# Filler products of the first batch, placed anew

## The chip, the cores and the metric

The kernel runs on one core of a Trainium2 chip. A core has five engines with an instruction queue each: TensorE (matrix products; PE in the profile, PEld its weight loads), VectorE (DVE), ScalarE (ACT), GpSimd (POOL) and SyncE (SP, which here only issues transfers). The metric is the time of one execution on the device in microseconds (us), lower is better; the time of a kernel is the median of several executions.

## The reference

It is a retention layer followed by a Fourier mixing block, for batch 4, 8 heads, 768 positions and head size 64:

```python
# attention: a decaying state for each head, y = scale * q . state
gamma = 1.0 - 2.0 ** (-5.0 - np.arange(H))
for t in range(S):
    state = gamma[None, :, None, None] * state + einsum('bhd,bhe->bhde', k[:, :, t], v[:, :, t])
    y[:, :, t] = scale * einsum('bhd,bhde->bhe', q[:, :, t], state)
x = y.transpose(0, 2, 1, 3).reshape(B, S, H * D)      # 4 x 768 x 512
# mixing and a two-layer network
u = x + real(fft(fft(x, axis=1), axis=2))
un = (u - mean(u)) / sqrt(var(u) + 1e-6)
out = u + maximum(un @ w_ch1, 0) @ w_ch2              # 512 -> 2048 -> 512
```

## The kernel before

The four batches go through the same stages one after the other. In the attention of a batch the eight heads are four pairs, numbered 0 to 3, and the 768 positions are six chunks of 128. The Fourier transforms are products with cosine and sine tables (`csp`, `ssp`, `cd16`, `sd16`), which the kernel computes itself at the start. Then comes the network, in halves of 384 rows.

While a later batch's attention runs, TensorE has the network of the batch before as dense work. The first batch has nothing of that kind beside it: its attention runs while the inputs arrive and while the tables are made. Its work is therefore written out by hand as one long list, `first_units()` (L1216): each entry is a small unit that issues some instructions on one engine, and `pin()` (L108) makes every engine keep exactly the order of the list. So a unit on an engine waits for all units of that engine that stand ahead of it, and beyond that only for its inputs and for free buffers.

The units that matter here, in the order in which a pair passes through them:

- `q0_unit`, `k0_unit`, `v0_unit` (L436 to L472) convert a pair's loaded q, k and v to 16 bits; the last letter names the engine (P for GpSimd, V for VectorE, A for ScalarE). The twelve loads themselves (L189) stand in SyncE's queue from the start.
- `t0_unit(i, part)` (L483): six TensorE transposes of q (part 0) or k (part 1); `te_unit` (L492, L495) copies the result, qTz or kT, out of PSUM on ScalarE or VectorE.
- `am_unit(i, half)` (L509): six products kT with qT into two wkA tiles; `ae_unit` (L516, VectorE) scales and masks them into atm.
- `kv0_unit` (L531): ten products of k and v into wkK; `sc_unit` (L540, VectorE) scans them into the running state s.
- `yi_unit` (L559) and `yx_unit` (L571): the products with atm and with the state that make y (wkY); `x0_unit` (L337, L339) writes y, scaled, to x.
- `trig` and `t_act` (L301 to L330) build the tables between these units, on ScalarE, VectorE and GpSimd; `mir_s`, `mir_d`, `turn_d` mirror them.
- `fold_s`, `fold_d`, `s1a_pre`, `s1b_pre`, `s1_mm`, `s1a_fin`, `s1b_fin` (L724, L738, L791, L839): the folds of x and the first Fourier products, after which TensorE's dense work begins (`px_unit`, `s2e_unit`, `h0_unit`, `ch_unit`).
- `w1_unit` and `w2_unit` (L1167, L1174) issue the eight transfers of the network's weights from GpSimd's queue. The loads of batch 1 (`load_unit`, L169) stand in SyncE's queue behind the seventh of them and behind a product of the first batch's network.

A filler is a product that nobody reads: `filler(n)` (L152) multiplies a tile of zeros, 128 x 128 by 128 x 512, n times into a PSUM tile of its own, `wps`. It waits for nothing but the zeros, written once at the start, and nothing waits for it, except the TensorE instructions that stand behind it in the queue. Six fillers are issued ahead of the list (L215), and six single ones stand in the list.

Of the kernel before, what the change touches and what calls it, by code (L numbers as in the profile page):

```python
# [18 lines left out]
P = 128  # L19
# [26 lines left out]
def kernel(  # L46
# [105 lines left out]
    def filler(n):  # L152
        def run():
            for _ in range(n):
                nc.tensor.matmul(wps, wz[:, 0:P], wz, start=True, stop=True)
        return run
# [138 lines left out]
    def trig(idx, part, eng):  # L295
        n, w, c = (S, SW, idx) if idx < 3 else (DM, DW, idx)
        r, ra = rs[2 * idx][:, 0:w], rs[2 * idx + 1][:, 0:w]

        def run():
            if part == 0 and eng == "A":  # L300
                nc.scalar.activation(ra, kf[:, 0:w], AF.Copy, bias=MAGIC, scale=icoln[:, c:c + 1])  # L301
            elif part == 0:
                eng_of(eng).tensor_scalar(out=ra, in0=kf[:, 0:w], scalar1=icoln[:, c:c + 1],
                                          scalar2=MAGIC, op0=ALU.mult, op1=ALU.add)
            elif part == 1:
                eng_of(eng).tensor_scalar(out=ra, in0=ra, scalar1=-MAGIC, scalar2=float(n),
                                          op0=ALU.add, op1=ALU.mult)
            else:
                eng_of(eng).scalar_tensor_tensor(out=r, in0=kf[:, 0:w], scalar=icol[:, c:c + 1],
                                                 in1=ra, op0=ALU.mult, op1=ALU.subtract)  # L310
        return run
# [124 lines left out]
    def q0_unit(i):  # L436
        def run():
            q16 = q16_of[0, i] = qzs[i % 2].rearrange("p h c d -> p (h c d)")[
                :, 0:NCH * P].rearrange("p (c h d) -> p c h d", c=NCH, h=2)
            nc.gpsimd.tensor_scalar(out=q16, in0=in_of.pop(("q", 0, i)).rearrange(  # L440
                "p h c d -> p c h d"), scalar1=1.0, scalar2=1.0, op0=ALU.mult, op1=ALU.mult)
        return run

    def k0_unit(i, h2, eng="P"):
        def run():
            h = 2 * PAIR_ORDER[i] + h2
            if h2 == 0:
                kd_of[0, i] = kp.tile([P, NCH, 2, D], f16, tag="kd16", name="kd16")
            k32, kd = in_of["k", 0, i][:, h2], kd_of[0, i][:, :, h2, :]
            if eng == "A":  # L450
                nc.scalar.activation(kd, k32, AF.Copy, bias=0.0, scale=gkd[:, h:h + 1])
            else:
                (nc.vector if eng == "V" else nc.gpsimd).tensor_scalar(
                    out=kd, in0=k32, scalar1=gkd[:, h:h + 1], scalar2=1.0, op0=ALU.mult,
                    op1=ALU.mult)
        return run
# [17 lines left out]
    def t0_unit(i, part):  # L474
        def run():
            if part == 0:
                at[0, i] = dict(kT=tp.tile([P, NCH, P], f16, tag="kT", name="kT"),
                                qT=qts[i % 2][:, 0])
            src = (q16_of, kd_of)[part][0, i]
            tq = at[0, i]["tq", part] = ps_g.tile([P, NCH, P], f16, tag="g", name="tq",  # L480
                                                  padded_shape=[P, 8, P])
            for c in range(NCH):
                nc.tensor.transpose(tq[:, c, :], src[:, c].rearrange("p a b -> p (a b)"), ident16)  # L483
        return run
# [730 lines left out]

    def first_units():  # L1216
        return [
            filler(1), trig(0, 0, "V"), trig(2, 0, "A"), k0_unit(0, 0, "V"), trig(1, 0, "V"),
            k0_unit(0, 1, "A"), q0_unit(0), t0_unit(0, 0), t0_unit(0, 1), te_unit(0, 0, "A"),
            filler(1), icoln_unit, te_unit(0, 1, "V"), am_unit(0, 0), trig(3, 0, "A"),  # L1220
            trig(4, 0, "A"), trig(4, 1, "P"), trig(2, 1, "P"), q0_unit(1), t0_unit(1, 0),
            trig(0, 1, "V"), k0_unit(1, 0, "P"), gk_unit(0), trig(0, 2, "V"), trig(2, 2, "V"),
            t_act(2, 0), k0_unit(1, 1, "A"), trig(1, 1, "P"), ae_unit(0, 0, 1), am_unit(0, 1),
            trig(4, 2, "V"), t_act(4, 2), v0_unit(0, 0, 6, "P"), parity_a, t_act(2, 2),
            filler(1), t0_unit(1, 1), trig(1, 2, "V"), kv0_unit(0), v0_unit(1, 0, 6, "P"),
            ae_unit(0, 1, 1), yi_unit(0, 1), t_act(0, 0), t_act(2, 1), sc_unit(0),
            te_unit(1, 1, "A"), te_unit(1, 0, "A"), am_unit(1, 0), am_unit(1, 1), t_act(0, 1),
            trig(3, 1, "V"), q0_unit(2), ae_unit(0, 1, 0), gk_unit(1), filler(1), kv0_unit(1),
            ae_unit(1, 0, 1), trig(3, 2, "V"), x_edges(1), t_act(4, 0), ae_unit(0, 0, 0),
            ae_unit(1, 1, 0), sc_unit(1), t_act(3, 2), yi_unit(0, 0), k0_unit(2, 0, "A"),  # L1230
            yx_unit(0), x0_unit(0, 0, "A"), t0_unit(2, 0), x0_unit(0, 1, "A"),
            k0_unit(2, 1, "P"), t0_unit(2, 1), te_unit(2, 1, "A"), ae_unit(1, 1, 1), yx_unit(1),
            te_unit(2, 0, "V"), t_act(1, 0), q0_unit(3), mir_d(1, "P"), t_act(1, 1),
            ae_unit(1, 0, 0), yi_unit(1, 0), x0_unit(1, 0, "V"), am_unit(2, 0), ae_unit(2, 0, 1),
            yi_unit(1, 1), x0_unit(1, 1, "A"), am_unit(2, 1), t0_unit(3, 0), ae_unit(2, 1, 0),
            mir_s(0, "P"), ae_unit(2, 1, 1), filler(1), te_unit(3, 0, "V"),
            fold_s(0, 0, 258, 0, 1, (1,), "V"), k0_unit(3, 0, "A"), k0_unit(3, 1, "P"),
            t0_unit(3, 1), te_unit(3, 1, "A"), am_unit(3, 0), w1_unit(0), v0_unit(2, 0, 3, "P"),
            fold_s(0, 0, 258, 0, 1, (0,), "V"), ae_unit(2, 0, 0), filler(1),
            v0_unit(2, 3, 6, "A"), minus_unit("A"), kv0_unit(2), t_act(3, 0), yi_unit(2, 0),  # L1240
            am_unit(3, 1), ae_unit(3, 0, 1), t_act(1, 2), t_act(4, 1), sc_unit(2), t_act(0, 2),
            v0_unit(3, 0, 3, "A"), yx_unit(2), x0_unit(2, 0, "A"), s1a_pre(0), yi_unit(2, 1),
            x0_unit(2, 1, "A"), w1_unit(1), ae_unit(3, 0, 0), v0_unit(3, 3, 6, "P"), kv0_unit(3),
            ae_unit(3, 1, 0), t_act(3, 1), ae_unit(3, 1, 1), yi_unit(3, 1), s1b_pre(0),
            turn_d(1, "P"), mir_s(1, "A"), yi_unit(3, 0), sc_unit(3), w1_unit(2), w1_unit(3),
            yx_unit(3), s1b_pre(1), s1a_pre(1), fold_s(0, 0, 130, 1, 2, (0,), "V"),
            fold_s(0, 0, 130, 1, 2, (1,), "V"), fold_d(0, 0, (0,), "V"), s1_mm(0), parity_b,
            x0_unit(3, 0, "A"), fold_d(0, 0, (1,), "V"), s1_mm(1), x0_unit(3, 1, "A"),
            fold_s(0, 130, 258, 1, 2, (0,), "V"), s1a_fin(0),
            fold_s(0, 130, 258, 1, 2, (1,), "V"), s1b_fin(0), s1a_fin(1), g_unit(0, "V"),  # L1250
            mir_d(0, "A"), turn_d(0, "P"), g_unit(1, "A"), s1b_fin(1), px_unit(0),
            s2e_unit(0, 0, (0,)), ga_unit("V"), xmean_unit(0), gb_unit(0, "V"), gr_unit(1, "V"),
            s2e_unit(0, 1, (0,)), s2e_unit(0, 0, (1,)), s2e_unit(0, 1, (1,)), gb_unit(1, "V"),
            px_unit(1), un0_unit(0, 0, "A"), unT0(0, 0), ut0(0, 0, "A"), w2_unit(0),
            xmean_unit(1), s2e_unit(1, 0, (1,)), s2e_unit(1, 1, (1,)), un0_unit(0, 1, "V"),
            unT0(0, 1), s2e_unit(1, 0, (0,)), second, s2e_unit(1, 1, (0,)), ut0(0, 1, "V"),
            h0_unit(0, 0), px_unit(2), s2e_unit(2, 0, (1,)), un0_unit(1, 2, "V"), unT0(1, 2),
            s2e_unit(2, 0, (0,)), ut0(1, 2, "A"), s2e_unit(2, 1, (0,)), w2_unit(1),
            xmean_unit(2), h0_unit(0, 2), w2_unit(2), s2e_unit(2, 1, (1,)), g0_unit(0, (0,)),
            h0_unit(1, 0), w2_unit(3), h0_unit(1, 2), un0_unit(2, 2, "V"), h0_unit(0, 1),  # L1260
            h0_unit(1, 3), h0_unit(1, 1), gr_unit(3, "A"), unT0(2, 2), ut0(2, 2, "A"),
            h0_unit(0, 3), h0_unit(2, 3), gr_unit(2, "A"), gr_unit(0, "V"), h0_unit(2, 1),
            h0_unit(2, 0), csn_unit(0, "V"), h0_unit(2, 2), csn_unit(1, "P"), g0_unit(0, (1,)),
            g0_unit(0, (2,)), u0_unit(0, 0, "V"), u0_unit(2, 2, "V"), u0_unit(0, 1, "A"),
            u0_unit(1, 2, "A"),
        ]
# [89 lines left out]
```

## Time and profile before

| | |
|---|---|
| time, median of 3 runs | 250.89 us (250.26 to 252.18) |
| profiled execution: its own time | 251.03 us |
| profiled execution: span from first to last instruction | 249.0 us |
| mean granted TensorE clock over the span | 0.973 |
| TensorE busy | 234.2 us, 94% of the span |
| VectorE, ScalarE, GpSimd busy | 174.2, 123.7, 81.0 us |
| fillers (wps, L155) | 12, from 2.0 to 23.7 us, 379 to 634 ns each |

The profile is of one execution. Instructions are named by engine, line of the kernel, operation, and the tiles written and read; a row gives the start in us from the start of the span, the time from its first start to its last end, the count, and in brackets the idle time of the engine before it and what ended it. Matrix products are pipelined: a row's time contains the whole length of its last product, so the distance between products is found from rows of several. The granted clock is the share of TensorE's full rate that the chip let it have; it comes with the windows, beside the busy time of each engine. The chain of waits is followed back from the last instruction, at each step to whatever released it.

### The profile page before, as it was taken

What the parts mean: (1) busy time and instruction counts of PE and PEld (TensorE: products, weight loads), DVE (VectorE), ACT (ScalarE), POOL (GpSimd) and SP (SyncE); (2) the same over time, 40 slices, a digit from 0 to 9 for tenths busy, and PEclk for the clock granted to TensorE, in tenths of its full rate; (3) what the DMA queues carried; (4) which work ended last, traced back from release to release, by engine and by line L of the source; (5) the groups of instructions that cost most, each with busy time, mean ns of one, the idle gap of its engine ahead of it and who ended that gap; (6) DMA issues with size and microseconds to landing.
All of it is one profiled execution on the core that took longest, in us unless ns stands there. A gap on an engine that the chain in (4) does not pass through costs nothing.

```text
span 249.0 us, 5322 instructions
## 1 busy us (share of the span) xinstructions
PE 234.2 (94%) x2041; PEld 146.8 (59%) x2041; DVE 174.2 (70%) x415; ACT 123.7 (50%) x278; POOL 81.0 (33%) x148
## 2 busy tenths in 40 slices
PE   6686999998899998999999999999999999999995
PEld 2364789844666565665567545665557455545543
DVE  4889874788979977988787745986886638323212
ACT  6767865556896445582246423751356406503400
POOL 5566370028910037874000452790001403100000
PEclk9759799999999999999999999999999999999999
DMA  7996999999959948968999768666200241221012
GB/s 191 252 244 93 188 189 191 212 247 254 271 122 210 227 110 180 176 139 133 249 260 227 136 116 231 121 123 153 87 0 3 42 144 25 47 81 46 0 45 84
DMA packets 99209, 36.39 MB, mean 146 GB/s; under 512 B 89840, under 2 KB 96240, under 8 KB 99184
## 3 DMA queue, kind: packets, MB, share of 16 engines
q1 hardware_dynamic: 94960, 31.86, 60.0%
q0 software_dynamic: 4224, 4.19, 10.7%
q8 instruction: 16, 0.26, 0.4%
q14 instruction: 9, 0.07, 0.1%
HBM read 27.26 MB, written 6.29 MB: 135 GB/s over the span
## 4 chain that ended last, share of the span: by engine, by line
PE 74%; DVE 7%; DMA 6%; ACT 5%; POOL 4%; SPq 2%; issue 2%; ACTq 0%; DVEq 0%
PE psc L1153 29%; PE psh L1109 22%; PE psh L1126 4%; DMA unT<-un 3%; PE ps L856 2%; PE wkA L645 2%; DMA k<-in_k_dram 2%; DVE atm L516 2%; PE wkY L699 2%; PE wkY L695 1%; DMA v<-in_v_dram 1%; ACT kT L612 1%; POOL u L1057 1%; PE pq L1027 1%; ACT un L1070 1%
## 5 line engine op out<-in xcount | busy, mean ns | idle before, releaser
L1153 PE MATMUL psc<-w,ht 128*128 128x512 f16 (+2 forms) x400 | 88.3, 370 | 0.0
L1109 PE MATMUL psh<-unT,w 128*128 128x384 f16 x448 | 81.8, 326 | 0.7 <-DVE ht L1115 0.4
L1153 PEld LDWEIGHTS <-ht 128*128 128x128 f16 x400 | 37.9, 98 | 38.1
L1109 PEld LDWEIGHTS <-w 128*128 128x128 f16 x448 | 42.4, 98 | 25.3 <-issue 2.0
L1113 ACT ACTIVATE ht<-psh 128x384 f16<-128x384 f32 x70 | 34.0, 490 | 46.9 <-PE psh L1109 46.5
L1055 POOL TENSOR_TENSOR u<-u,x 128x256 f32<-128x256 f32 x21 | 13.3, 634 | 112.6 <-DVE u L1034 94.9
L1157 DVE SCALAR_TENSOR_TENSOR ob<-psc,stats,u 128x512 f32<-128x512 f32 (+2 forms) x25 | 18.1, 723 | 26.4 <-PE psc L1153 26.3
L1115 DVE TENSOR_SCALAR ht<-psh 128x384 f16<-128x384 f32 x42 | 22.9, 551 | 9.9 <-PE psh L1109 9.5
L648 DVE TENSOR_TENSOR atm<-wkA,maskp 128x512 f16<-128x512 f32 x36 | 24.1, 683 | 1.8 <-PE wkA L645 1.8
L1070 ACT ACTIVATE un<-u,stats 128x512 f16<-128x512 f32 x21 | 15.2, 722 | 15.8 <-DVE stats L1069 10.6
L1068 DVE BATCH_NORM_STATS2 bst<-u 128x6 f32<-128x512 f32 x21 | 14.6, 695 | 8.6 <-POOL u L1057 8.6
L674 DVE SCALAR_TENSOR_TENSOR s<-s,gk,wkK 128x128 f16<-128x128 f16 x48 | 16.1, 336 | 2.0 <-ACT s L670 1.4
L707 ACT ACTIVATE x<-wkY,gexp 128x384 f16<-128x384 f32 x24 | 12.8, 581 | 7.5 <-PE wkY L699 7.4
L1057 POOL TENSOR_TENSOR u<-u,x 128x256 f32<-128x256 f32 x21 | 13.3, 635 | 4.8 <-DVE u L1037 3.0
L425 POOL TENSOR_SCALAR kd<-k,gexp 128x384 f16<-128x384 f32 x24 | 13.8, 585 | 0.0
L645 PE MATMUL wkA<-qTz,kT 128*128 128x256 f16 x72 | 13.1, 272 | 0.0
L1126 PE MATMUL psh<-unT,w 128*128 128x128 f16 x192 | 11.4, 219 | 0.0
L1126 PEld LDWEIGHTS <-w 128*128 128x128 f16 x192 | 11.0, 98 | 0.1
L430 POOL TENSOR_SCALAR v<-v 128x768 f16<-128x768 f32 x12 | 10.0, 830 | 0.0
L1034 DVE SCALAR_TENSOR_TENSOR u<-pq,g,qn 128x256 f32<-128x256 f32 x18 | 8.5, 470 | 1.7 <-PE psh L1109 0.9
L645 PEld LDWEIGHTS <-kT 128*128 128x128 f16 x72 | 6.8, 98 | 4.6
L724 DVE TENSOR_TENSOR xab<-x 128x780 f16<-128x780 f16 (+4 forms) x18 | 8.8, 526 | 0.8 <-ACT x L337 0.4
(187 smaller groups left out, 320.7 us busy)
## 6 DMA issues: line engine op xcount, KB each, us to landing
q<-in_q_dram SPq DMA_DIRECT2D x16, 384.0 KB, 5.9
k<-in_k_dram SPq DMA_DIRECT2D x16, 384.0 KB, 5.7
v<-in_v_dram SPq DMA_DIRECT2D x16, 384.0 KB, 6.2
out_dram<-ob SPq DMA_DIRECT2D x23, 256.0 KB, 2.4
w<-in_moe_w_ch_dram POOLq DMA_DIRECT2D x8, 512.0 KB, 9.4
unT<-un SPq DMA_TRANSPOSE x15, 2.4
out_dram<-ob SPq DMA_DIRECT2D x1, 192.0 KB, 1.9
qTz<-q16z SPq DMA_TRANSPOSE x8, 3.8
```

The source lines that it names most:

```text
L645: mm = nc.tensor.matmul(wk[:, c2], st["kT"][:, c, :], st["qT"][:, :, c, :], start=True, stop=True)
L648: nc.vector.tensor_tensor(out=st["atm"][:, 2 * part:2 * part + 2], in0=wk, in1=maskp[:, PAIR_ORDER[i]].unsqueeze(1).to_broadcast([P, 2, 2, ...
L674: nc.vector.scalar_tensor_tensor(out=s16[:, c], in0=s16[:, c - 1], scalar=gk2[:, hp:hp + 1], in1=wk[:, c - c0], op0=ALU.mult, op1=ALU.add)
L1057: nc.gpsimd.tensor_tensor(out=u[:, kb, 256:512], in0=u[:, kb, 256:512], in1=x[:, kb, 1, 257:1:-1], op=ALU.add)
L1068: nc.vector.bn_stats(bst, u[:, kb, :])
L1070: nc.scalar.activation(un, u[:, kb, :], AF.Identity, bias=stats[:, kb, 0:1], scale=-1.0)
L1109: nc.tensor.matmul(psh, w116[:, cb, fb * P:(fb + 1) * P], unT[:, cb, rt * 384:(rt + 1) * 384], start=(cb == 0), stop=(cb == 3))
L1113: nc.scalar.activation(ht16[:, fb, :], psh, AF.Relu, bias=0.0, scale=-1.0)
L1115: nc.vector.tensor_scalar(out=ht16[:, fb, :], in0=psh, scalar1=-1.0, scalar2=0.0, op0=ALU.mult, op1=ALU.max)
L1126: mm = nc.tensor.matmul(psh[:, f], w116[:, cb, fb * P:(fb + 1) * P], unT[:, cb, kb * P:(kb + 1) * P], start=(cb == 0), stop=(cb == 3))
L1153: nc.tensor.matmul(psc[:, c0:c1], ht16[:, fb, rb3 * P:(rb3 + 1) * P], w216[:, fb, c0:c1], start=(fb == 0), stop=(fb == NFB - 1))
L1157: nc.vector.scalar_tensor_tensor(out=ob[:, c0:c1], in0=psc[:, c0:c1], scalar=lb[b]["st"][:, rb, 3:4], in1=lb[b]["u"][:, rb, c0:c1], op0=AL ...
```

## The change

One list changes: in `first_units()` the six single fillers are taken out and thirteen new calls of `filler` with counts from 1 to 7 are put in, 47 products together. The six fillers ahead of the list stay. All other units, and their order, stay as they are; no wait, buffer or transfer is added or taken away.

```diff
     def first_units():
         return [
-            filler(1), trig(0, 0, "V"), trig(2, 0, "A"), k0_unit(0, 0, "V"), trig(1, 0, "V"),
-            k0_unit(0, 1, "A"), q0_unit(0), t0_unit(0, 0), t0_unit(0, 1), te_unit(0, 0, "A"),
-            filler(1), icoln_unit, te_unit(0, 1, "V"), am_unit(0, 0), trig(3, 0, "A"),
...
+            trig(0, 0, "V"), trig(2, 0, "A"), k0_unit(0, 0, "V"), trig(1, 0, "V"),
+            k0_unit(0, 1, "A"), q0_unit(0), filler(7), t0_unit(0, 0), filler(5), t0_unit(0, 1),
+            te_unit(0, 0, "A"), icoln_unit, te_unit(0, 1, "V"), filler(4), am_unit(0, 0),
...
```

The list has some 150 entries. TensorE's order before and after, up to the first Fourier products, with F for a filler:

| before | after |
|---|---|
| 6 F, then 1 F ahead of t0(0,0) | 6 F, then 7 F ahead of t0(0,0) |
| - | 5 F ahead of t0(0,1) |
| 1 F ahead of am(0,0) | 4 F ahead of am(0,0) |
| - | 3 F ahead of t0(1,0) |
| 1 F ahead of t0(1,1) | 2 F ahead of t0(1,1) |
| - | 3 F ahead of kv0(0) |
| - | 4 F ahead of am(1,0) |
| 1 F ahead of kv0(1) | 2 F ahead of kv0(1) |
| - | 2 F ahead of yi(0,0) |
| 1 F ahead of t0(3,1) | 6 F ahead of t0(3,1) |
| - | 4 F ahead of am(3,0) |
| 1 F ahead of kv0(2) | - |
| - | 4 F ahead of yx(2) |
| - | 1 F ahead of yi(3,1) |

In the trace before, these units start on TensorE at: t0(0,0) 5.14, t0(0,1) 6.63, am(0,0) 7.79, t0(1,0) 9.52, t0(1,1) 11.11, kv0(0) 12.18, am(1,0) 13.54, kv0(1) 15.93, yi(0,0) 16.61, t0(3,1) 22.02, am(3,0) 23.42, kv0(2) 24.02, yx(2) 26.04, yi(3,1) 27.93 us.

## The prediction

> **What bounds the kernel now.** I read the page first: TensorE is busy 94% of the span and carries 74% of the chain that ended last, so time won or lost on its way to the dense stage stays won or lost. Section 2 shows where TensorE is not at full speed: only in the first five slices of 6.2 us.
>
> ```profile
> span 249.0 us, 5322 instructions
> PE   6686999998899998999999999999999999999995
> PEclk9759799999999999999999999999999999999999
> PE 74%; DVE 7%; DMA 6%; ACT 5%; POOL 4%; SPq 2%; issue 2%; ACTq 0%; DVEq 0%
> ```
>
> Next the windows of the first stage, cut where the granted clock changes. Quarter-microsecond windows put the changes at 8.89 (down), 19.13 (up), 25.95 (down) and 29.37 us (up); after that it stays up. The distances are 10.24, 6.82 and 3.42 us, so the clock is judged in steps of 3.41 us, and I cut the table at these steps. Columns: window, its length, then busy time (and count) of PE, weight loads, DVE, ACT, POOL; clock, DMA share, GB/s.
>
> ```profile
> 2.06:5.47 3.41, 3.41 (x11) 1.14 (x12) 1.46 (x5) 1.97 (x7) 2.12 (x13) 1.00 1.06 265
> 5.47:8.89 3.42, 1.39 (x18) 0.71 (x16) 2.15 (x7) 2.80 (x7) 0.95 (x3) 1.00 1.26 260
> 12.30:15.71 3.41, 2.54 (x29) 1.54 (x29) 2.68 (x6) 2.29 (x6) 2.15 (x5) 0.50 1.24 256
> 15.71:19.13 3.42, 3.42 (x47) 2.62 (x48) 2.91 (x5) 1.99 (x5) 1.61 (x3) 0.50 1.36 231
> 19.13:22.54 3.41, 2.63 (x45) 1.62 (x41) 2.96 (x7) 2.48 (x5) 1.88 (x3) 1.00 0.60 102
> 22.54:25.95 3.41, 1.69 (x29) 1.03 (x30) 3.41 (x7) 2.80 (x7) 3.33 (x6) 1.00 0.70 99
> ```
>
> Each window decides the next one's clock. One with TensorE busy 1.39 or 1.69 us of 3.41 is followed by half clock; the full one (15.71) by full clock; 2.63 us left it up, 2.54 us left it down. The 1.00 of the first line is no reading: the fillers there are slow, as their row shows.
>
> ```profile
> 1.98 3.17 PE L155 MATMUL wps<-ht 128*128 128x512 f16 x7 [1.98 <-POOL ht L214]
> 6.63 0.51 PE L483 MATMUL tq<-ident,kd 128*128 128x128 f16 x6 [0.84 <-DVE tmp L303]
> 18.12 0.84 PE L483 MATMUL tq<-ident,kd 128*128 128x128 f16 x6
> 23.42 0.34 PE L509 MATMUL wkA<-qTz,kT 64*128 64x128 f16 x6 [0.89 <-ACT kT L495]
> ```
>
> Seven fillers in 3.17 us, the last of 0.61: (3.17-0.61)/6 = 0.427 us apart, against 0.216 for the 512-wide products of the dense stage. Six transposes take 0.84 us slow and 0.51 fast. The six at 5.14 took 0.65, so the clock rose among them, one step before 8.89: at 5.47. Last, the chain of waits of the first 34 us:
>
> ```profile
> 5.96 0.61 ACT kd L451
> 8.70 0.97 DVE tmp L309
> 9.67 0.47 DVE atm L516
> 12.18 0.77 PE wkK L531 x10
> 15.46 0.54 PE wps L155
> 17.57 0.77 PE tq L483 x6
> 18.36 0.96 DVE qTz L492
> 26.04 0.53 PE wkY L571 x10
> 28.43 0.65 PE psB L791 x6
> ```
>
> It goes k's load, ACT, DVE to 12.1; mostly TensorE, slow, to 18.3; DVE almost gapless to 26.0; TensorE, slow until 29.4, then fast and dense. So **the clock costs in two stretches only**, 12.2 to 18.3 and 26.0 to 29.4 us; elsewhere fillers can only be hidden or be late.
>
> **The change, step by step.** Six single fillers of the list go, 47 come (the six issued ahead of the list stay). No operation is new; a filler costs 0.427 us slow, 0.216 fast, and TensorE runs in order, so a filler that isn't done when the next input arrives delays it. I walk along the real work, naming how much later (+) or earlier (-) it starts than in the trace.
>
> *Start: 13 fillers before the first transposes, instead of seven.* From 1.98 eight slow ones reach 5.39, the ninth meets the rise at 5.47 (0.25), four fast ones 0.86: 6.50, where the transposes started at 5.14: **+1.36**. Five fillers follow: 6.50+0.34+1.08 = 7.92 against 6.63, **+1.29**; the wait for kd (6.58) is covered. DVE's kT copy moves from 7.18 to 8.47 and four fillers end at 9.12, so the first wkA products come at 9.12 against 7.79. What is late next is DVE's queue: kT, three index operations, atm. Its 0.25 us wait for POOL before 8.70 takes some of it (ACT's qTz moves only 0.5, from 6.48 to 7.0, and POOL's part with it), so atm and all that follows on DVE come about **+1.0**: from 8.70 to 12.12 DVE has no idle time to give. The three and two fillers before the next transposes and the three before wkK (0.65 us) lie beside that.
>
> *First recovery, if the clock stays up.* The wkK products (12.18) take 0.47 us as at 24.02 and not 0.74: the scan that waits for them is at +0.75, and the wkA products that waited for DVE at 14.98 too. The four fillers before wkA of pair 1 (13.54) make it about +1.2, but its reader on DVE starts only at 14.85+0.75, so that hides. Then TensorE leads: from wkA to wkK (14.98 to 15.93) 0.95 with one slow filler becomes 0.22+0.43 = 0.65, **-0.30**; wkK to wkY 0.68 becomes 0.33 and two fillers 0.43, **+0.08**; wkY to the next 0.43 becomes 0.20, **-0.23**; those strided ones 0.46 to 0.42; six transposes and the rest of their pipe to DVE's qTz copy 0.86 to 0.55, **-0.31**. Sum 0.75-0.80: the copy of 18.36 is at **-0.05**.
>
> *DVE's stretch, 18.36 to 26.0.* It moves as a block, about 0. Six fillers at 21.29 (1.30 us for a gap of 0.73) make the kd transposes +0.57 and wkA 23.42 the same; its reader (24.72) has over 0.3 us to spare. POOL's queue has the weight issues (L1167, 21.91) behind a mirror that waits for ACT, which waits for the transposes of 18.12: they come 0 to 0.4 earlier, no queue later. No filler issues a DMA; SP's loads of batch 1 wait for the seventh weight piece (it lands at 45.47), and so move with POOL's queue alone.
>
> *Second recovery.* Four fillers (0.86) before the wkY products of 26.04, where the gap was 0.57: +0.12. From there everything is fast: to psA 0.41, to wkY 0.18, to wkK 0.20, so wkK is at 26.95 against 27.25; its scan, 0.54 after its start instead of 0.79, at 27.5 against 28.04; the products that need it at 28.36 against 29.34 (the single filler lies in that wait): **-0.98**. Then x, the folds and s1 on DVE take some back: s1 products at 29.5 and 30.1 against 30.33 and 30.85, the last fold's at 30.62 against 31.40: **-0.8**.
>
> *From there to the end.* In every two-microsecond window from 30 to 58 TensorE is busy 2.0, so the lead is carried. The weight pieces it meets have landed well before: the third at 34.14 for use at 37.1, the last at 48.06 for about 51.5. One load has little to spare: the last v of batch 1 lands at 68.42 for POOL at 68.70; its products come later, and I price it at 0 to 0.3.
>
> Sum: 251.03 (the profiled execution; span 249.0 and 2.0 around it) - 0.8 = **250.2**. The median, 250.89, is 0.14 below that execution; the forecast for either is the same to within what the steps can bear.
>
> A measurement of this kernel can tell about 1% from no change.
>
> **The rivals.**
>
> *The clock falls at 15.7 all the same (slower).* After the change TensorE is busy some two thirds of 12.30 to 15.71 (fast wkK, wkY, wkA, four fillers and six more at the ends, but waits for DVE remain, 14.0 to 14.5 and 15.1 to 15.7). 1.69 of 3.41 dropped the clock, 2.63 kept it; two thirds, 2.25, lies between, nearer the upper. If it falls, the run to 18.3 is slow again: +0.75 at its start, the two fillers before wkK 0.86 instead of 0.54 (+0.32), two more before wkY +0.86, with 0.3 back when the window ends: +1.6 on DVE's stretch; less 0.75 of the second recovery, +0.85: **251.9**. It decides from a busy share between 0.50 and 0.77 in that window.
>
> The Trainium skill, TensorE: Matmul & The Clock Gate, Part 1, says that the clock falls after a whole idle window and advises only against gaps above some 3 us. By that this rival could not be, and the sum would stay 250.2. The trace disagrees: the clock fell at 8.89 and 25.95 with no gap above 1.4 us in the window before.
>
> *The steps of the clock lie elsewhere.* This execution was lucky: a step began at 2.06, just as the fillers did (1.98). If it began later, up to all 13 run slow: 1.98+13x0.427 = 7.53, another 1.03 later; the first atm is then near +2.0, and with the same two recoveries the end is +0.2: **251.2**. The three times before, 1.9 us apart, leave room for such a difference between executions.
>
> The Trainium skill, TensorE: Matmul & The Clock Gate, Part 1, calls the window free-running, so that the start varies from run to run; the step of 3.41 us in the trace agrees, one execution can't show the phase.
>
> *The start costs nothing.* If the loads or ACT hold the first atm back by more than I see, the 1.0 us vanishes: -1.8, **249.2**. For it speaks only the wait for k, against it that DVE is full from 8.70.
>
> *It doesn't do what it says:* the fillers count for nothing and the clock goes as before. Then +1.0 at the start, +1.2 before wkK and wkY, +0.1 at 26.0 and 0.43 for the single one: **253.7**. Against it: the fillers of 2.06 to 5.47 alone raised the clock.
>
> **How the numbers follow.** Forecast 0.45, clock falls 0.20, other phase 0.15, free start 0.12, nothing 0.08. The range goes from the free start less a spread of 0.8, 248.4, to 253.0, which holds the fall with 1.1 above it and cuts the last rival. Faster by over 1% (below 248.4) takes the best of the free start and a little of the forecast: 0.10. Slower by over 1% (above 253.4): the last rival and the worst of the fall, two windows slow: 0.13. Same 0.77. With both signs open, the forecast's own range is 249.4 to 251.0.
>
> **What would show it.** Right: clock up from about 5.5 us without a break; the first transposes near 6.5, DVE's first atm near 10.6, the qTz copy of 18.36 within 0.3 of its place, the wkY products of 29.34 near 28.4, s1 about 0.8 early. The forecast is wrong if the granted clock drops anywhere after 9 us, if the first atm is under +0.5 or over +1.5, or if the lead of the s1 products isn't there at the last output.

## The result, and the profile after

Over 20 executions of each kernel the change takes 250.38 us (249.81 to 251.44) against 252.18 us before (250.26 to 253.02). The ratio is 0.9945, with a 95% interval of 0.9925 to 0.9965: about 1.4 us, 0.9 to 1.9, faster. The forecast was 0.8 us faster, 250.2 us, and the time lies in its range. But the profile of the change looks odd beside that: its execution took 251.32 us and its span is 249.2, longer than the 249.0 of the profiled execution before. A gain in the median and a loss between the two profiles: this is what the experiments had to explain.

The page of the kernel after; the lines answer to those shown of before (span, TensorE's busy tenths, the clock, the chain by engine and, new here, by line):

```profile
span 249.2 us, 5404 instructions
...
PE   6989999999899998999999999999999999999995
...
PEclk9999999999999999999999999999999999999999
...
PE 76%; DVE 9%; POOL 5%; ACT 3%; issue 2%; DMA 1%; SPq 1%; POOLq 0%; DVEq 0%; ACTq 0%
PE psc L1153 29%; PE psh L1109 23%; PE psh L1126 4%; PE wps L155 3%; PE ps L856 2%; PE wkA L645 2%; DVE atm L516 2%; POOL u L1057 2%; PE wkY L699 2%; DMA v<-in_v_dram 1%; PE wkY L695 1%; DVE bst L1068 1%; ACT kT L612 1%; DVE tmp L309 1%; PE pq L1027 1%
```

Once up, the clock never drops, as was forecast; the mean clock of all 20 executions is 0.998 to 1.000. But the fillers, wps, now hold 3% of the chain, and TensorE's rows show where it begins (start, time, engine and line, operation, tiles, count; the first two rows of the kernel after):

```profile
1.97 5.73 PE L155 MATMUL wps<-ht 128*128 128x512 f16 x13 [1.97 <-POOL ht L214]
7.49 0.56 PE L483 MATMUL tq<-ident,q16z 128*128 128x128 f16 x6
```

All 13 fillers are slow: 1.97 + 13 x 0.427 = 7.52. The first transposes start at 7.49, not at the 6.50 of the forecast, because in this execution the clock rose only at 7.60 (the first clock record of the trace; the 1.00 of the page ahead of it is no reading). The windows of the kernel after, cut at this execution's own steps of 3.41 us (window, length, busy time of PE, weight loads, DVE, ACT, POOL; clock, DMA share, GB/s), show why it stays up:

```profile
7.60:11.02 3.42, 3.42 (x31) 1.79 (x29) 1.48 (x3) 1.90 (x4) 1.46 (x4) 1.00 1.24 255
11.02:14.43 3.41, 2.89 (x35) 1.53 (x33) 3.05 (x9) 2.27 (x7) 2.73 (x5) 1.00 1.33 232
14.43:17.85 3.42, 3.06 (x43) 1.43 (x38) 3.11 (x6) 2.62 (x7) 2.27 (x5) 1.00 1.24 261
17.85:21.26 3.41, 2.81 (x48) 1.97 (x48) 3.05 (x6) 2.77 (x6) 0.48 (x1) 1.00 1.11 184
```

TensorE is busy 2.81 us or more of every step. Set against the profiled execution before, the first stage runs so:

| starts on | before | after | shift |
|---|---|---|---|
| TensorE: first q transposes (L483) | 5.14 | 7.49 | +2.35 |
| VectorE: first atm (L516) | 9.59 | 11.77 | +2.18 |
| VectorE: copy of qTz of pair 2 (L492) | 18.36 | 19.50 | +1.14 |
| VectorE: scan of pair 2 (L540) | 25.18 | 26.39 | +1.21 |
| TensorE: wkY of pair 3 with the state (L571) | 29.34 | 29.92 | +0.58 |
| TensorE: first px product (L937) | 32.46 | 33.19 | +0.73 |

The stage wins time back twice, as the forecast worked out, but it starts from 2.2 us late instead of 1.0, and ends 0.73 us late instead of 0.8 early. Yet the whole time is only 0.29 longer. The rest lies far behind the stage, at TensorE's products of 150 us (the first row is of the execution before, the second of the one after):

```profile
150.50 2.11 PE L1109 MATMUL psh<-unT,w 128*128 128x384 f16 x12 [0.22 <-DMA unT<-un]
150.80 2.11 PE L1109 MATMUL psh<-unT,w 128*128 128x384 f16 x12
```

Before, TensorE waits there for a transposing transfer; after, it does not.

### The profile page after: what moved, and what is told of

The parts are those of the page before. It is cut to its first block, busy times and chain, and to the rows that moved or that the text cites. A ratio compares the mean times of both kernels' runs of the same rounds, so it can differ in the third digit from the quotient of the medians.

```text
span 249.2 us, 5404 instructions
## 1 busy us (share of the span) xinstructions
PE 239.4 (96%) x2082; PEld 147.7 (59%) x2082; DVE 173.9 (70%) x415; ACT 123.4 (50%) x278; POOL 81.2 (33%) x148
## 4 chain that ended last, share of the span: by engine, by line
PE 76%; DVE 9%; POOL 5%; ACT 3%; issue 2%; DMA 1%; SPq 1%; POOLq 0%; DVEq 0%; ACTq 0%
PE psc L1153 29%; PE psh L1109 23%; PE psh L1126 4%; PE wps L155 3%; PE ps L856 2%; PE wkA L645 2%; DVE atm L516 2%; POOL u L1057 2%; PE wkY L699 2%; DMA v<-in_v_dram 1%; PE wkY L695 1%; DVE bst L1068 1%; ACT kT L612 1%; DVE tmp L309 1%; PE pq L1027 1%
## 5 line engine op out<-in xcount | busy, mean ns | idle before, releaser
L1153 PEld LDWEIGHTS <-ht 128*128 128x128 f16 x400 | 37.9, 98 | 38.1
L155 PE MATMUL wps<-ht 128*128 128x512 f16 x53 | 16.4, 442 | 2.0 <-POOL ht L214 2.0
L155 PEld LDWEIGHTS <-ht 128*128 128x128 f16 x53 | 5.0, 109 | 7.6 <-issue 3.0
```

Source lines behind the costliest of these rows:

```text
L1153: nc.tensor.matmul(psc[:, c0:c1], ht16[:, fb, rb3 * P:(rb3 + 1) * P], w216[:, fb, c0:c1], start=(fb == 0), stop=(fb == NFB - 1))
```

## The experiments

Theory A: what fillers run past the arrival of the next input is carried through VectorE's queue to the end of the stage, and the full clock wins time back where TensorE leads (so far the forecast), and where the steps of the clock lie differs between executions (in the forecast a rival). The rivals are named with each run. The first px product (L937; 32.46 us in the first trace before, 33.19 after) marks the end of the stage. Ratios are to the kernel before, taken anew beside each set of runs; its medians there are 251.48 to 251.57 us, against the 252.18 of the first comparison.

**The kernel before, once more.** No edit.

> The kernel before, unchanged, in another execution. Theory A (the steps of the clock lie anywhere relative to the start): rise and fall stand at other times than 5.47, 8.89, 19.13, 25.95 and 29.37 us, still whole steps of 3.41 us apart, and the first px product moves with them within 32.2 to 33.7 us (32.46 in the first profile), the span by as much. Rival (the steps are tied to the start): the same times within 0.1 us.

It took 252.68 us. The clock rose first at 31.40 us, and never before. TensorE's rows of this execution (columns as above):

```profile
1.98 3.17 PE L155 MATMUL wps<-ht 128*128 128x512 f16 x7 [1.98 <-POOL ht L214]
5.13 0.82 PE L483 MATMUL tq<-ident,q16z 128*128 128x128 f16 x6
6.59 0.82 PE L483 MATMUL tq<-ident,kd 128*128 128x128 f16 x6 [0.64 <-DVE tmp L303]
```

The same seven fillers at the same time, but the transposes behind them take 0.82 us, slow, where the first trace had 0.65 and 0.51. Here a step began near 4.1 us, and no step was filled before the one from 27.99 us on. The first px product came at 33.62, 1.16 later, and the time is 1.65 us longer; the wait for the transposing transfer near 150 us is there again, now 0.70 us. So the steps are not tied to the start. Neither trace is the rule by itself. For 63 further executions of the kernel before, taken beside the experiments, the mean clock is on record; the time ahead of the first rise counts as full in it. It is 0.958 to 0.986 in 44: there the clock rose early and fell again, as in the first trace. In the other 19 it is 0.998 or more, which is what an execution shows whose clock rises once and stays, early or, as here, only at 31 us. The first profile before was on the lucky side: of the 83 executions on record, 22 are faster than its 251.03 us.

**The kernel after, once more.** No edit.

> The kernel after the change, unchanged, in another execution. Theory A: the clock rises between 5.4 and 8.8 us (7.60 in the first profile) and never falls; the first transposes start at 6.5 to 7.5 us, and the first px product at 31.6 to 33.2, later the later the clock rises. Rival (tied to the start): 7.60 and 33.19 again within 0.1 us.

250.85 us; clock up at 6.94 and never down; first transposes at 7.23, first px product at 32.70. Against the first trace of it (7.60, 33.19, 251.32 us) the clock rises 0.66 earlier, the first px product comes 0.49 earlier and the time is 0.47 less. In both executions the time behind the first px product is the same, 250.85 - 32.70 = 218.15 and 251.32 - 33.19 = 218.13.

**One filler instead of seven at the start.**

```diff
-            k0_unit(0, 1, "A"), q0_unit(0), filler(7), t0_unit(0, 0), filler(5), t0_unit(0, 1),
+            k0_unit(0, 1, "A"), q0_unit(0), filler(1), t0_unit(0, 0), filler(5), t0_unit(0, 1),
```

> The change with one filler instead of seven ahead of the first transposes, the other 40 as in the change. Theory A (TensorE's queue carries the delay: what the fillers run past 5.14 us sets back the whole first stage, and the full clock wins it back later): the first transposes start near 5.1 instead of 7.49, VectorE's first atm at 9.7 to 10.8 instead of 11.77, the first px product 1.0 to 1.6 us earlier than after the change (31.6 to 32.2 against 33.19); in the time 1.0 to 1.5 us under the change, ratio to before 0.987 to 0.991. Theory B (the late start is absorbed by the waits for loads, ScalarE and VectorE that follow): time as after the change, ratio 0.994 within 0.002. Theory C (the seven are what brings the clock up in time): without them the clock rises only at 15 to 19 us and the time is that of before or above, ratio 0.999 to 1.006.

248.83 us, ratio to before 0.990 (0.9875 to 0.9925), 1.1 us under the change by the two ratios, 1.55 by the medians. Rows of TensorE:

```profile
1.98 3.17 PE L155 MATMUL wps<-ht 128*128 128x512 f16 x7 [1.98 <-POOL ht L214]
5.02 0.69 PE L483 MATMUL tq<-ident,q16z 128*128 128x128 f16 x6
...
30.65 0.41 PE L937 MATMUL pq<-x,ident 128*128 128x256 f16 x3
```

In this execution the clock rose at 5.44, as in the first trace before, and did not fall. The first transposes are at 5.02, the first px product at 30.65: 1.81 earlier than in that trace, which had the same first rise but the singles of before. Against the change's two traces it is 2.54 and 2.05 earlier, more than the 1.0 to 1.6 expected, as their first transposes are 2.47 and 2.21 later. Theory A holds; the seven are not needed to bring the clock up (theory C), and their delay is not absorbed (B).

**Twelve instead of seven at the start**: the same cost the other way.

```diff
-            k0_unit(0, 1, "A"), q0_unit(0), filler(7), t0_unit(0, 0), filler(5), t0_unit(0, 1),
+            k0_unit(0, 1, "A"), q0_unit(0), filler(12), t0_unit(0, 0), filler(5), t0_unit(0, 1),
```

> The change with twelve fillers instead of seven ahead of the first transposes: the suspected cost of the start, five products more. Theory A (the start is carried to the end): five products of 0.216 to 0.427 us each, 1.1 to 1.6 us, in the first transposes (8.3 to 9.6 us) and as much at the first px product and in the time: 251.3 to 252.1, ratio 0.998 to 1.002. Rival (the start is absorbed by the waits behind it): time as after the change, ratio 0.993 to 0.996.

252.28 us, ratio 1.0032 (1.001 to 1.0054): slower than before. As the clock rose early in this execution (6.09), the first transposes start at 7.89, earlier than the 8.3 to 9.6 expected, and the first px product at 33.91. Against the change the time is +1.9 us by the medians and +2.2 by the ratios, over the expected 1.1 to 1.6. The start is carried nearly whole: from the first transposes to the first px product it is 26.02 us here, 25.63 with one filler, and 25.70 and 25.47 in the two traces of the change.

**Only the late fillers**: the list of before up to the second pair's transposes, the change's from wkK on.

```diff
-            ... filler(7), t0_unit(0, 0), filler(5), t0_unit(0, 1), ... filler(4), am_unit(0, 0),
-            ... filler(3), t0_unit(1, 0), ... filler(2), t0_unit(1, 1), ...
+            ... filler(1), t0_unit(0, 0), t0_unit(0, 1), ... filler(1), am_unit(0, 0),
+            ... t0_unit(1, 0), ... filler(1), t0_unit(1, 1), ...
```

> The list of before up to the second pair's transposes (single fillers ahead of the first transposes, the first wkA products and the second k transposes), and the change's 31 fillers from the first wkK products on. Theory A: no start delay; the clock comes up one or two steps later than after the change (between 9 and 19 us) but then stays; first px product at 31.4 to 32.5, time 0.3 to 1.2 us under the change, ratio 0.987 to 0.993. Theory B: the early fillers are needed to win; ratio 0.997 to 1.001.

250.56 us, 0.9958 (0.994 to 0.9975): faster than before, but by less than theory A expected, and level with the change. No start delay (first transposes at 4.95), but the clock stays up only from 12.89 on. Windows of its trace:

```profile
6.06:9.47 3.41, 1.23 (x16) 0.73 (x17) 2.64 (x8) 2.10 (x5) 1.55 (x4) 1.00 1.31 241
9.47:12.89 3.42, 3.42 (x24) 1.72 (x24) 1.83 (x7) 3.18 (x8) 1.77 (x3) 0.50 1.23 264
```

A step with 1.23 us busy costs the clock for the next one, in which the single fillers and the three ahead of wkK are slow; wkK starts at 12.84, +0.66. The early fillers do hold the clock; it is the number at the very start that costs.

**Only the early fillers**: the change up to wkK, then the three single ones of before.

```diff
-            ... filler(4), am_unit(1, 0), ... filler(2), kv0_unit(1), ... filler(2), yi_unit(0, 0),
-            ... filler(6), t0_unit(3, 1), ... filler(4), am_unit(3, 0), ... filler(4), yx_unit(2),
-            ... filler(1), yi_unit(3, 1),
+            ... am_unit(1, 0), ... filler(1), kv0_unit(1), ... yi_unit(0, 0),
+            ... filler(1), t0_unit(3, 1), ... am_unit(3, 0), ... filler(1), kv0_unit(2), ... yx_unit(2),
+            ... yi_unit(3, 1),
```

> The change's 24 fillers up to the first wkK products, then the three single ones of before. Theory A: the start delay of 1.4 to 2.4 us is paid and little of it won back, since the clock falls again at 15 to 26 us: ratio 1.003 to 1.007, first px product 33.0 to 34.8. Theory B (the early fillers win by themselves): ratio 0.994 to 0.998.

251.45 us, 0.9988 (0.9961 to 1.0015): no gain, as A has it, though not the loss of 0.3 to 0.7% that I expected; why it is less was not traced. The clock rose at 6.77, fell at 17.01 and again at 27.25, after these steps:

```profile
13.60:17.01 3.41, 2.21 (x40) 1.41 (x39) 2.77 (x8) 3.09 (x8) 2.66 (x6) 1.00 1.23 266
...
23.84:27.25 3.41, 2.12 (x41) 1.35 (x39) 3.41 (x8) 3.26 (x8) 3.37 (x6) 1.00 0.92 140
```

**No filler in the list.** The six ahead of it stay.

> No filler in the list at all; the six issued ahead of it stay. Theory A: the six singles of before were worth about nothing, since they change no step of the clock by much and stand in gaps: ratio 0.997 to 1.001, the clock at half over most of 9 to 29 us as before. Theory B (fillers always help): slower than before, ratio 1.002 to 1.006.

251.53 us, 1.000 (0.9976 to 1.0024). In its trace the clock rose first at 31.80 us. The six single fillers of before did nothing for the time that can be measured: the change's gain does not come from taking them away.

**The first experiment without its middle fillers.**

```diff
-            ... filler(4), am_unit(1, 0), ... filler(2), kv0_unit(1), ... filler(2), yi_unit(0, 0),
+            ... am_unit(1, 0), ... kv0_unit(1), ... yi_unit(0, 0),
```

> The kernel of the first experiment (the change with one filler instead of seven at the start, 248.83 us) without its eight fillers ahead of the wkA, wkK and wkY products between 13 and 16 us. Theory A (the clock of each 3.41 us step is decided by the busy share of the step before; the middle fillers keep it up): the share of a step between 11 and 18 us falls from about 3.0 of 3.41 us to 2.2 to 2.6, and the clock falls for at least one step: time 1.0 to 2.5 us over the first experiment, ratio to before 0.994 to 1.000. Theory B (only a longer idle gap drops the clock, as the longest gap stays under 1 us): the clock stays up and the time is at or a little under the first experiment's, ratio 0.987 to 0.991.

250.80 us, 0.9962 (0.9928 to 0.9996), against 248.83 with them. This is the forecast's slower rival, made on purpose, in its windows:

```profile
11.60:15.02 3.42, 2.13 (x40) 1.34 (x38) 2.79 (x7) 2.66 (x6) 1.41 (x2) 1.00 1.30 233
15.02:18.43 3.41, 2.79 (x44) 2.15 (x40) 3.24 (x6) 2.00 (x5) 2.24 (x6) 0.50 1.28 254
18.43:21.84 3.41, 3.00 (x41) 2.04 (x36) 2.60 (x6) 2.50 (x5) 1.86 (x3) 0.50 0.89 147
```

2.13 us busy, and the clock is down for three steps, to 25.25: once slow, 2.79 and 3.00 us are not enough to bring it back. The longest gap in the step that dropped it was 0.41 us, so a long gap is not needed (theory B falls). The ten executions sort themselves by the clock: 249.21 and 249.34 us at a mean clock of 0.998, 249.44 at 0.993, 250.19 to 250.81 at 0.985 or 0.986, 251.84 to 252.19 at 0.980; the traced one is of the last kind. Eight fillers of 0.22 us, 1.7 us of work that nobody reads, are worth 1.6 us here by the ratios, 2.0 by the medians.

**Fewer at the start, moved to where there is room.** Two, one, four, four ahead of the first four groups; two ahead of the first wkY; three ahead of the wkY of 26 us.

```diff
-            ... filler(7), t0_unit(0, 0), filler(5), t0_unit(0, 1), ... filler(3), t0_unit(1, 0),
-            ... yi_unit(0, 1), ... filler(4), yx_unit(2), ... filler(1), yi_unit(3, 1),
+            ... filler(2), t0_unit(0, 0), filler(1), t0_unit(0, 1), ... filler(4), t0_unit(1, 0),
+            ... filler(2), yi_unit(0, 1), ... filler(3), yx_unit(2), ... yi_unit(3, 1),
```

> The change with two fillers instead of seven ahead of the first q transposes, one instead of five ahead of the first k transposes, four instead of three ahead of the second pair's q transposes, two new ones ahead of the first wkY products, three instead of four ahead of the wkY products of 26 us, and none ahead of the last wkY products with atm. Theory A (late fillers at the start are the only loss that is left): the first px product 30.2 to 31.0 us whatever the step of the clock, time 248.0 to 248.8 us, ratio to before 0.985 to 0.989, below the first experiment's 0.990 and with less spread. Rival: with so few at the start the clock comes up one step later in part of the executions, ratio 0.990 to 0.994.

248.82 us, 0.9906 (0.987 to 0.9941): the first experiment's time, no better, and one of its six executions took 250.49. In the trace the clock rose at 7.21, half a step later than in the first experiment, and yet the first px product is at 30.65 in both: a later rise cost nothing here. But the spread of the times isn't smaller (248.69 to 250.49, against 248.51 to 249.65), the expected gain over the first experiment isn't there, and the ratio lies where the rival put it. The execution of 250.49 us has a mean clock of 0.992 against 0.999 or more in the others, as if one step had run at half clock; no trace shows which.

**Fewer late ones too.** The first experiment's chain runs through fillers from 20 us on; the three longest pieces:

```profile
20.34 1.29 PE wps L155 x6
...
21.96 0.86 PE wps L155 x4
...
24.15 0.97 PE wps L155 x4
```

```diff
-            ... filler(6), t0_unit(3, 1), ... filler(4), yx_unit(2), ... filler(1), yi_unit(3, 1),
+            ... filler(3), t0_unit(3, 1), ... filler(2), yx_unit(2), ... yi_unit(3, 1),
```

> The kernel of the first experiment (the change with one filler instead of seven at the start) with three fillers instead of six ahead of the last k transposes, two instead of four ahead of the wkY products of 26 us, and none ahead of the last wkY products with atm. In the first experiment's trace the chain runs through these fillers (1.29, 0.97 and 0.32 us), while their inputs are there 0.7, 0.4 and 0.3 us earlier. Theory A (what a filler runs past the input's arrival is carried, until VectorE's queue leads): the first px product 0.3 to 0.5 us earlier than in the first experiment (30.65 there), time 248.2 to 248.6, ratio 0.986 to 0.990. Rival (these fillers held the clock): a step between 19 and 26 us falls under 2.2 to 2.6 us busy, the clock falls and the time is 249.5 to 251.

248.38 us, 0.9889 (0.9855 to 0.9923), the lowest of all; the first px product at 29.91, 0.74 earlier than in the first experiment (0.3 to 0.5 expected), and the clock, once up at 6.10, stays up. Its interval and the first experiment's overlap: that it is the faster of the two is seen in one trace of each, not shown by the times. It beats both the change and the kernel before.

## Why the prediction was right or wrong

*What came out.* The median moved the way that was forecast, and 250.38 is near 250.2. The clock, once up, stayed up, and the stage loses time at the start and wins some back twice. But of the signs that the forecast named, only the clock's holding came out in the traced executions: the first atm is +2.18 and +1.85, beyond the +1.5 at which it called itself wrong; the qTz copy of 18.36 is at +1.14 and +0.53, for within 0.3; and the first px product behind s1 is 0.73 and 0.24 late, where s1 should be 0.8 early. That the time is right all the same is in part luck, as the terms show.

*The start.* The step that failed is "the ninth meets the rise at 5.47", and with it the +1.36 for the first transposes. It took the rise of one execution for that of the next. In the two executions traced after the change the clock rose at 7.60 and 6.94 and the shift was +2.35 and +2.09. The rival "the steps of the clock lie elsewhere" is what happened there; its 7.53 for the first transposes was measured at 7.49. Its +0.2 for the end is close to 251.32 - 251.03 = +0.29 in the time, but not by its own sum, since the stage ended at +0.73. Both traced executions are slower than the median of 250.38. Seven of the 20 took under 250.0 us; where the clock rose in them is not on record.

*What the comparison was with.* The sum took the profiled execution's 251.03 for the kernel's time and read the spread of the first three as noise. Twenty executions have their median at 252.18, and the 63 later ones at 251.52: the change wins 1.4 us against the first set and would win 1.1 against the second, where the forecast counted 0.8 against one of the better executions.

*VectorE's queue.* I let 0.36 of the start be absorbed by the wait for POOL; measured, 2.35 became 2.18, so only 0.17. The wait itself is gone (VectorE has no idle ahead of that tmp row, L309, any more); but qTz on ScalarE, which POOL's part follows, moved by 1.61 (6.48 to 8.09), where I had put 0.5.

*The first recovery* has the right sum: 1.05 us by the working, from the first atm to the copy of qTz; measured 2.18 - 1.14 = 1.04. Its parts were other ones. Up to the first scan 0.25 was forecast, and 0.47 came (13.03 to 14.74); from there on 0.80, and 0.57 came. I had TensorE lead in the second part; in the chain of the kernel after, VectorE's instructions follow each other without a gap from that scan to 20.91, so its queue set the limit:

```profile
18.40 0.73 DVE s L540
19.13 0.45 DVE atm L516
19.57 0.87 DVE qTz L492
```

*VectorE's stretch* moved as a block, +1.14 to +1.21, as said.

*The second recovery* was oversized: 0.75 by the working from there to the end of s1, measured 1.21 - 0.73 = 0.48. The term that was wrong is the four fillers before the wkY products of 26 us, "+0.12"; the two numbers it stands beside, 0.86 for the fillers and 0.57 for the gap, already differ by 0.29. The chain of the kernel after has

```profile
26.41 0.27 PE wkA L509 x6
26.68 0.97 PE wps L155 x4
27.65 0.46 PE wkY L571 x10
...
28.97 0.32 PE wps L155
```

and the shift goes from +1.21 to +1.54 there: 0.33. The last single one, which I had put beside a wait, is on the chain as well (0.32). The experiment with fewer late fillers, which halves the four and drops the single one, ended its stage 0.74 earlier than the first one.

*Carried to the end.* The shift is 0.68 to 0.73 in every row from 33 to 149 us, so what the stage ends with is carried. At 150.5 it becomes +0.30, by the wait for the transposing transfer that is gone. The forecast had no term for it. The wait is in all three traces of kernels without the change's fillers (0.22, 0.70 and, with no filler in the list, 0.5 us) and in none of the nine with early or late ones, so it is a part of the gain: behind the first px product the kernel before takes 218.57 and 219.06 us, the change 218.13 and 218.15. Why the transfer lands earlier was not tested. An estimate of what this does to the forecast: with its own start, first transposes at 6.50, and the 25.63 from there to the first px product of the run with one filler, the stage would end at 32.13, only 0.33 early; with 218.14 behind it the time is 250.3. So the forecast's 0.8 would be reached, but more than half of it by a wait that the forecast did not have.

*The clock falls at 15.7.* It did not. I had put TensorE's share of that step at 2.25 us; the steps there measure 2.89 and 3.06. The limits, 1.69 and 2.63, were sound, and the mechanism is real: 2.13 us dropped the clock in the run without middle fillers. By the Trainium skill, TensorE: Matmul & The Clock Gate, Part 1, table of the two states, the clock falls after a whole idle window. The runs disagree: it fell after steps of 2.12 to 2.21 us busy whose longest gaps were 0.41 to 0.89 us.

*It doesn't do what it says* and *the start costs nothing*: neither. The runs with twelve, seven and one at the start (252.28, 250.38, 248.83 us) show the start carried nearly whole.

## What to carry to other kernels

Work without a reader can pay if it holds the clock for a stage in which TensorE leads, but it belongs into the gaps that remain at the fast rate: what a filler runs past the next input's arrival is carried on, here nearly whole from the start of the stage to its end, and at half clock each costs twice (0.427 us against 0.216). Before a change of this kind is priced, take several executions: where the steps of the clock lie makes one trace a draw, and the first trace here was a better one than most. And follow a shift to the last output: here a wait 120 us behind the changed stage went away with the change.

## What the runs showed of the hardware

- The steps of 3.41 us lie differently against the start in each execution: the first rise stood at 5.47 us or at 31.40 in the kernel before, at 7.60 or 6.94 in the change. The kernel before spreads over 2.8 us in 20 executions, the change over 1.6; how much of that the steps make is not known beyond the two traces of each.
- The fall: in the first stage, steps with TensorE busy 1.23 to 2.21 us of 3.41 were followed by half clock, steps with 2.34 or more never (2.34 in the run with twelve at the start, 2.63 and up elsewhere). But later, in the network, steps with 2.18 (from 60.09 us, first trace before), 2.22 (57.30, fewer late ones) and 2.23 us (58.40, fewer at the start) kept the full clock. So the line lies near 0.65 of a step, and the busy time alone doesn't settle the cases close to it.
- The rise: at half clock a step filled to 3.41 us brought the full clock back every time. Below that the busy time doesn't tell: 3.00 and 3.23 us (14.73, no filler in the list) and 3.36 (24.58, second trace before) did not bring it back; 2.81 (1.36, without middle fillers), 3.13 (2.65, only late ones) and 3.33 us (25.95, first trace before) did. The 2.81 and the 3.13 are first steps, made up mostly of the 512-wide fillers. What is counted there is open.
